# Moving later loads to the GpSimd queue, and the transposes of q and k behind those of u, in an attention and MLP-mixer kernel

## The chip, the cores and the metric

The kernel runs on one core of one Trainium2 chip. The metric is the device time of one execution in microseconds (us). A single core has no second die to compare with, so a run counts as slow here when it is over 1.5% above the fastest of the same kernel; only fast runs are compared. The kernels were run in rounds that alternate with the kernel before on the same chip. Runs of different experiments can come from different chips; a ratio always compares with the kernel before in the same rounds. TensorE, VectorE, ScalarE, GpSimd and SyncE appear in the profile as PE, DVE, ACT, POOL and SP; PEld is TensorE's weight load, and a q behind a name (SPq, ACTq) means work of that engine's sequencer, such as issuing a DMA.

## The reference, cut to what matters

Windowed attention with 4 sink keys, then an MLP mixer, on 4 batches. Everything is float32 outside and bf16 inside.

```python
# q, k, v: (4 batches, 8 heads, 768, 64); n_sink = 4, window = 128
scores = q @ k.T / 8, kept where key < 4 or 0 <= query - key < 128
x = softmax(scores) @ v                      # heads side by side: (4, 768, 512)
u = x + (relu(x.T @ w_tok1) @ w_tok2).T      # tokens:   768 -> 256 -> 768
out = u + relu(u @ w_ch1) @ w_ch2            # channels: 512 -> 1536 -> 512
```

## The kernel before

The batches are pipelined. While TensorE does the channel products of batch b (`ch1`, `ch2`: the "main" stream), the attention and the token products of batch b + 1 are put in between (the "fill"), each at a fraction of the main stream's length. A batch has two groups of four heads, so groups 0 to 7; batch 1 is groups 2 and 3, batch 2 groups 4 and 5, batch 3 groups 6 and 7. From batch 1 on, u is transposed by six DMA transposes (128 x 512 bf16, 128 KB each), and from batch 2 on q and k of each group by one DMA transpose each (128 x 1536 bf16, 384 KB). In this text a "stage" is the stretch of one batch's main stream. All of the following go through the sync queue, where the traces show them issued in program order (in the kernel before the transposes of u, whose input was written by 92.9 us, were issued from 112.6 us on, behind the six loads issued from 91.1 to 109.0): loads of groups 4 to 7, all DMA transposes, and all stores but one.

```python
def load_qk(eng, src, dst, G, lo, hi): ...
    # groups 4 to 7: one DMA of 768 KB, rows of 64 floats (256 bytes), 3072 rows
    eng.dma_start(out=dst.rearrange("p h t d -> p (h t) d"),
                  in_=src[G.b, G.h0:G.h0 + GH].rearrange("h (t p) d -> p (h t) d", p=P))

def cast_and_turn(G, which, copy):           # groups 4 to 7
    ...                                      # GpSimd casts q or k to bf16
    T = att.tile([P, 2 * NT, P], BF16, name="qT" if which == 0 else "kT")
    nc.sync.dma_start_transpose(out=T, in_=flat)

def utr(st):                                 # u of batch 1, 2, 3
    nc.sync.dma_start_transpose(out=uT[:, :, ts(st, P)], in_=u_sb[:, st])

def ch1(half, ft):                           # first product of a stage: needs uT of st 0, 1, 2
    ps = ps_mx.tile([P, HS], FP32, name="ps_v", tag="mx")   # two PSUM buffers
    for c in range(NC):
        nc.tensor.matmul(ps, w_ch1[:, c, ts(ft, P)], uT[:, c, ds(half * HS, HS)], ...)
    # even ft: ScalarE empties PSUM, odd ft: VectorE

# ---- cut ----
def fetch(g):                                # on the sync queue
    G = held[g] = tiles(g)
    load_q(G, 0, GH); load_k(G, 0, GH); load_v(G)

def prep_v(g):
    cast_v(held[g])                          # GpSimd; frees the buffer that v of g + 2 needs
    if g + 2 < NG and g >= 2:
        fetch(g + 2)

# ---- cut: the fill of stage b, for batch b + 1 (groups g, h) ----
    lo, mid = (0.36, 0.80) if b == 0 else (0.02, 0.68)      # attention of batch b + 1
    ...
    if b + 2 < B:
        fill += [(mid + 0.01, lambda n=n: prep_qk(n)) for n in (h + 1, h + 2)]   # cast and turn
        fill += [(mid + 0.01, lambda n=n: prep_v(n)) for n in (h + 1, h + 2)]    # cast, then fetch
    hi = mid + 0.03                                         # u of batch b + 1 and its transposes
    fill += [(hi + (0.97 - hi) * n / (len(nhead) - 1), f) for n, (f, _) in enumerate(nhead)]
```

The attention of batches 2 and 3 begins with four small copies on ScalarE (`sink_keys`, L225 before, L229 after), which read kT of both groups before the first exponential.

The softmax here doesn't subtract the row's maximum and nothing guards it: scores larger than these inputs give would overflow.

Of the kernel before, what the change touches and what calls it, by code (L numbers as in the profile page):

```python
# [16 lines left out]
def kernel(  # L17
# [13 lines left out]
    nc = tc.nc  # L31
# [75 lines left out]
    def load_q(G, lo, hi, eng=nc.sync):  # L107
        return load_qk(eng, q, G.q32, G, lo, hi)
# [5 lines left out]
        src, dst = ((G.q32, G.qb), (G.k32, G.kb))[which]  # L114
        copy(dst[:, j].rearrange("p t i d -> p i t d"), src[:, 2 * j:2 * j + 2])

    def cast_and_turn(G, which, copy):
        src, dst = ((G.q32, G.qb), (G.k32, G.kb))[which]
        flat = dst.rearrange("p j t i d -> p (j t i d)")
        copy(flat.rearrange("p (t h d) -> p t h d", t=NT, h=GH), src.rearrange("p h t d -> p t h d"))  # L120
        T = att.tile([P, 2 * NT, P], BF16, name="qT" if which == 0 else "kT")
        nc.sync.dma_start_transpose(out=T, in_=flat)  # L122
        G.T[which] = [T.rearrange("d (t j) p -> d t j p", j=2)[:, :, j] for j in range(2)]

    def by_dve(o, i):
# [5 lines left out]
    def by_act(o, i):  # L131
        nc.scalar.activation(o, i, AF.Copy)

    def load_v(G):
        return nc.sync.dma_start(out=G.v32.rearrange("p h t d -> p (h t) d"),  # L135
                                 in_=v[G.b, G.h0:G.h0 + GH].rearrange("h (t p) d -> p (h t) d", p=P))

    def load_sinks():
# [179 lines left out]
    def mixer(b, x_b):  # L318
        h1 = mix.tile([P, NTOK, DM], BF16, name="h1")
        u_sb = mix.tile([P, NT, DM], BF16, name="u_sb")  # L320
        uT = mix.tile([P, NC, S], BF16, name="uT")
        v1 = mix.tile([P, NF, S], BF16, name="v1", bufs=1)
        st_ps = {}

        def tok1(a, tt):
            ps = ps_mx.tile([P, GH * D], FP32, name="ps_h", tag="mx")
            for t in range(NT):
                nc.tensor.matmul(ps, w_tok1[:, t, ts(tt, P)], x_b[:, t, ds(a * GH * D, GH * D)],  # L328
                                 start=(t == 0), stop=(t == NT - 1))
            nc.scalar.activation(h1[:, tt, ds(a * GH * D, GH * D)], ps, AF.Relu)  # L330

        def tok2(st):
            ps = ps_ms.tile([P, DM], FP32, name="ps_u", tag="ms")
            for tt in range(NTOK):
                nc.tensor.matmul(ps, w_tok2[:, tt, ts(st, P)], h1[:, tt], start=(tt == 0), stop=(tt == NTOK - 1))  # L335
            nc.vector.tensor_tensor(out=u_sb[:, st], in0=ps, in1=x_b[:, st], op=ALU.add)  # L336

        def utr(st):
            if b > 0:
                nc.sync.dma_start_transpose(out=uT[:, :, ts(st, P)], in_=u_sb[:, st])  # L340
                return
            ps = ps_ms.tile([P, NC, P], BF16, name="ps_ut", tag="ms")
            for c in range(NC):
                nc.tensor.transpose(ps[:, c], u_sb[:, st, ts(c, P)], ident)
            nc.scalar.activation(uT[:, :, ts(st, P)], ps, AF.Copy)

        def ch1(half, ft):
            ps = ps_mx.tile([P, HS], FP32, name="ps_v", tag="mx")
            for c in range(NC):
                nc.tensor.matmul(ps, w_ch1[:, c, ts(ft, P)], uT[:, c, ds(half * HS, HS)],  # L350
                                 start=(c == 0), stop=(c == NC - 1))
            if ft % 2 == 0:
                nc.scalar.activation(v1[:, ft, ds(half * HS, HS)], ps, AF.Relu)  # L353
            else:
                nc.vector.tensor_scalar(out=v1[:, ft, ds(half * HS, HS)], in0=ps, scalar1=0.0, scalar2=None, op0=ALU.max)  # L355

        def ch2(st, part):
            if part == 0:
                st_ps[st] = ps_mx.tile([P, DM], FP32, name="ps_w", tag="mx")
            ps = st_ps[st]  # L360
            for ft in range(4 * part, 4 * part + 4):
                nc.tensor.matmul(ps, v1[:, ft, ts(st, P)], w_ch2[:, ft], start=(ft == 0), stop=(ft == NF - 1))  # L362
            if part == NF // 4 - 1:
                o = osb.tile([P, DM], FP32, name="o")
                nc.vector.tensor_tensor(out=o, in0=ps, in1=u_sb[:, st], op=ALU.add)  # L365
                if b == B - 1 and st == NT - 1:
                    hw = DM // 2
                    nc.sync.dma_start(out=out[b, ds(st * P, P), 0:hw], in_=o[:, 0:hw])
                    nc.scalar.dma_start(out=out[b, ds(st * P, P), hw:DM], in_=o[:, hw:DM])
                else:  # L370
                    nc.sync.dma_start(out=out[b, ds(st * P, P)], in_=o)  # L371

        t1 = [[(lambda a=a, tt=tt: tok1(a, tt), 660) for tt in range(NTOK)] for a in range(GB)]
        T2 = lambda st: (lambda: tok2(st), 432)
        X = lambda st: (lambda: utr(st), 222)
        C1 = lambda h, f: (lambda: ch1(h, f), 650)
        C2 = lambda s, p: (lambda: ch2(s, p), 864)
        head = [T2(0), T2(1), X(0), T2(2), X(1), T2(3), X(2), T2(4), X(3), T2(5), X(4), X(5)]
        if b == 0:
            hf = NF // 2  # L380
            m = [T2(0), T2(1), X(0), T2(2), X(1), X(2), C1(0, 0), T2(3), C1(0, 1), X(3), T2(4), C1(0, 2), X(4), T2(5),
                 C1(0, 3), X(5)]
            m += [C1(0, f) for f in range(4, hf)] + [C1(1, f) for f in range(hf)]
            m += [C1(0, f) for f in range(hf, NF)] + [C1(1, f) for f in range(hf, NF)]
            m += [C2(s, p) for s in range(NT) for p in range(NF // 4)]
        else:
            m = [C1(0, f) for f in range(NF)]
            for n in range(3):
                m += [C1(1, f) for f in range(4 * n, 4 * n + 4)] + [C2(n, p) for p in range(NF // 4)]
            m += [C2(s, p) for s in range(3, NT) for p in range(NF // 4)]  # L390
        return t1, head, m
# [17 lines left out]
    with tc.manual_schedule():  # L409
# [4 lines left out]
            mixers[b] = mixer(b, xs[b])  # L414

        def fetch(g):
            G = held[g] = tiles(g)
            load_q(G, 0, GH)
            load_k(G, 0, GH)
            load_v(G)  # L420

        def prep_qk(g, by=(by_pool, by_pool)):
            if held[g].dma:
                for which in range(2):
                    cast_and_turn(held[g], which, by_pool)
                return
            for j in range(2):
                for which in range(2):
                    cast(held[g], j, which, by[which])

        def prep_v(g):
            cast_v(held[g])
            if g + 2 < NG and g >= 2:
                fetch(g + 2)

        def begin(g):
            parts[g] = attention(g, held[g], xs[g // GB], False)
# [40 lines left out]
        def more_loads():  # L478
            load_ch1(0)
            load_ch1(1)  # L480
            G = held[2] = tiles(2)
            load_q(G, 0, GH, nc.gpsimd)
            load_k(G, 0, GH, nc.gpsimd)
            load_ch2(0)
            load_ch2(1)
            G = held[3] = tiles(3)
            load_q(G, 0, GH, nc.gpsimd)
            last = load_k(G, 0, GH, nc.gpsimd)
            after(load_v(held[2]), last)
            load_v(G)  # L490

        idle(11)
        seq = [C(G0, 0, 0, by_dve), C(G0, 0, 1, by_act), zeros, step(0, 0, 0), step(0, 0, 1), I(1), step(0, 1, 0)]
        seq += [C(G0, 1, 0, by_pool), C(G0, 1, 1, by_pool), step(0, 0, 2), step(0, 1, 1), step(0, 0, 3), step(0, 1, 2)]
        seq += [C(G1, 0, 0, by_pool), C(G1, 0, 1, by_pool), I(1), step(0, 1, 3), step(1, 0, 0), step(0, 1, 4)]
        seq += [step(1, 0, 1), step(0, 1, 5), step(1, 1, 0)]
        seq += [C(G1, 1, 0, by_pool), C(G1, 1, 1, by_pool), step(0, 2, 0), step(1, 0, 2), step(1, 1, 1), step(1, 0, 3)]
        seq += [lambda: cast_v(G0), lambda: cast_sinks(0, GB), step(1, 1, 2), load_tok, step(1, 1, 3)]
        seq += [step(0, 3, 0), step(1, 1, 4), step(0, 3, 1), lambda: cast_v(G1), step(0, 3, 2), step(1, 2, 0)]
        seq += [step(1, 1, 5), step(0, 3, 3), step(0, 3, 4), step(0, 3, 5), more_loads, step(1, 4, 0)]  # L500
        seq += [f for f, _ in mixers[0][0][0]]
        seq += [step(1, 4, 1), step(1, 4, 2)]
        seq += [f for f, _ in mixers[0][0][1]]
        seq += [build_mask0, lambda: cast_sinks(GB, NG)]
        run(seq)

        for b in range(B):
            main, fill = mixers.pop(b)[2], []
            if b + 1 < B:
# [2 lines left out]
                nt1, nhead, _ = mixers[b + 1]  # L512
                order = []
                if b == 0:
                    order += [(lambda: prep_qk(2), 0)]
                order += [(lambda g=g: begin(g), 0)] + ([(lambda h=h: begin(h), 0)] if b > 0 else [])
                if held[g].dma:
# [15 lines left out]
                    order += [(step(g, 3, 2 * n), 6), (step(g, 3, 2 * n + 1), 6)]  # L533
                order += [(step(h, 2, 0), 8)] + [(f, 7) for f, _ in nt1[0]]
                order += [(step(h, 3, i), 6) for i in range(NT)] + [(f, 7) for f, _ in nt1[1]]
                lo, mid = (0.36, 0.80) if b == 0 else (0.02, 0.68)
                total, t = sum(w for _, w in order), 0
                for f, w in order:
                    fill.append((lo + (mid - lo) * t / total, f))
                    t += w  # L540
                if b + 2 < B:
                    fill += [(mid + 0.01, lambda n=n: prep_qk(n)) for n in (h + 1, h + 2)]
                    fill += [(mid + 0.01, lambda n=n: prep_v(n)) for n in (h + 1, h + 2)]
                hi = mid + 0.03
                fill += [(hi + (0.97 - hi) * n / (len(nhead) - 1), f) for n, (f, _) in enumerate(nhead)]
            run(spread(main, fill))
# [1 line left out]
_INS = ['q', 'k', 'v', 'n_sink', 'window', 'moe_w_tok1', 'moe_w_tok2', 'moe_w_ch1', 'moe_w_ch2']  # L548
# [31 lines left out]
```

## Time and profile before

| | before |
|---|---|
| median of the runs | 257.0 us (255.64 to 260.06, one of four slow) |
| span of the profiled run | 256.6 us |
| TensorE busy | 210.2 us, 82% |
| one TensorE wait for uT in stage 1 | 24.6 us |
| mean granted TensorE clock | 0.93 |

The first fence is from the page of the kernel before: the span, TensorE's busy time, then rows of 40 slices of 6.4 us each (the digit is the busy share in tenths; PEclk is the granted clock, DMA the mean busy share of the 16 DMA engines), then the DMA queues with packets, MB and the share of the engines' time. q1 is the queue of SyncE (hardware, as the page calls it), q0 that of GpSimd (software).

```profile
span 256.6 us, 3888 instructions
...
PE   8996859997998960005888999979799999999993
...
PEclk9999968999999997555999999997999999999999
DMA  6999999599499999997100149550001115401122
...
q1 hardware_dynamic: 76560, 26.22, 49.1%
q0 software_dynamic: 4576, 7.11, 12.6%
```

There is one large hole in TensorE's row, almost four slices wide (24.6 us), and the DMA row is nearly full in it. The list of waits of the kernel before (who waited for whom: us in total, times, longest) names it:

```profile
PE ps_v L350 <- DMA uT<-u_sb: 24.6, 1, 24.6
```

The timeline of the sync queue in the kernel before (start us, us, what) shows why uT is late. L122 are transposes of q and k, L103 and L135 loads, L371 a store, L340 the transposes of u:

```profile
83.30 1.78 SPq L122 DMA_TRANSPOSE qT<-qb  x1
...
89.36 1.64 SPq L122 DMA_TRANSPOSE kT<-kb  x1
91.06 0.98 SPq L103 DMA_DIRECT2D q_1248<-in_q_dram  x1
92.09 2.54 SPq L103 DMA_DIRECT2D k_1249<-in_k_dram  x1
94.73 3.47 SPq L135 DMA_DIRECT2D v_1252<-in_v_dram  x1
...
105.50 3.50 SPq L135 DMA_DIRECT2D v_1263<-in_v_dram  x1
109.09 3.46 SPq L371 DMA_DIRECT2D out_dram<-o  x1
112.64 2.52 SPq L340 DMA_TRANSPOSE uT<-u_sb  x2
...
115.84 5.15 SPq L340 DMA_TRANSPOSE uT<-u_sb  x4
```

VectorE wrote the last u of batch 1 by 92.9 us, but six loads of groups 6 and 7 stand in the queue ahead of its transposes. The view of the tile uT in the kernel before (from 85 to 130 us; first the issue times in ns, minimum, median and maximum) shows that the transposes themselves are quick:

```profile
L340 SPq DMA_TRANSPOSE uT<-u_sb x6: 1211/1216/1264, 112.6 to 119.8; - x6
...
DMA to landing us min/median/max: 2.4/2.5/3.8
```

The timeline of GpSimd in the kernel before, around the cast of v of group 3 (L200) and the masks of group 3 (L252 to L262):

```profile
67.48 1.46 POOL L200 CAST va<-v_470 128x1536 bf16<-128x1536 f32 x1
68.91 1.15 POOL L252 TENSOR_TENSOR pT<-pT,mask_92 128x512 bf16<-128x512 bf16 x1
...
76.49 0.64 POOL L262 TENSOR_SCALAR_AFFINE_SELECT pT<-pT 128x512 bf16<-128x512 bf16 x1
```

TensorE's attention output of group 3 (L280) starts at 77.25 us, 0.1 us behind the last mask: GpSimd has hardly any slack there.

### The profile page before, as it was taken

What the parts mean: (1) busy time and instruction counts of PE and PEld (TensorE: products, weight loads), DVE (VectorE), ACT (ScalarE), POOL (GpSimd) and SP (SyncE); (2) the same over time, 40 slices, a digit from 0 to 9 for tenths busy, and PEclk for the clock granted to TensorE, in tenths of its full rate; (3) what the DMA queues carried; (4) which work ended last, traced back from release to release, by engine and by line L of the source; (5) the groups of instructions that cost most, each with busy time, mean ns of one, the idle gap of its engine ahead of it and who ended that gap; (6) DMA issues with size and microseconds to landing.
All of it is one profiled execution on the core that took longest, in us unless ns stands there. A gap on an engine that the chain in (4) does not pass through costs nothing.

```text
span 256.6 us, 3888 instructions
## 1 busy us (share of the span) xinstructions
PE 210.2 (82%) x1547; PEld 112.7 (44%) x1565; DVE 107.0 (42%) x241; ACT 91.1 (36%) x152; POOL 91.1 (36%) x121
## 2 busy tenths in 40 slices
PE   8996859997998960005888999979799999999993
PEld 3444624554565520002445665434456644554441
DVE  5657644364746450000225473531344636333221
ACT  3794224469751000002775421065754200231100
POOL 8759322018999300000485980015654000000000
PEclk9999968999999997555999999997999999999999
DMA  6999999599499999997100149550001115401122
GB/s 231 320 195 178 233 293 260 183 210 228 94 216 229 241 212 218 218 231 160 43 0 3 41 96 191 147 143 0 3 0 43 41 43 135 111 0 43 41 82 82
DMA packets 82113, 34.88 MB, mean 136 GB/s; under 512 B 72544, under 2 KB 78432, under 8 KB 82096
## 3 DMA queue, kind: packets, MB, share of 16 engines
q1 hardware_dynamic: 76560, 26.22, 49.1%
q0 software_dynamic: 4576, 7.11, 12.6%
q10 hardware_dynamic: 960, 1.31, 1.5%
q8 instruction: 12, 0.20, 0.3%
q14 instruction: 5, 0.04, 0.1%
HBM read 26.77 MB, written 6.29 MB: 129 GB/s over the span
## 4 chain that ended last, share of the span: by engine, by line
PE 57%; SPq 12%; ACT 10%; DVE 8%; DMA 6%; POOL 3%; issue 2%; DVEq 0%; ACTq 0%; POOLq 0%
PE ps_v L350 20%; PE ps_w L362 18%; ACT pT L248 7%; SPq L103 4%; DMA v_948<-in_v_dram 4%; PE ps_s L242 3%; PE ps_u L335 3%; SPq L135 3%; PE ps_h L328 3%; DMA uT<-u_sb 2%; PE ps_warm L468 2%; SPq L122 2%; SPq L371 2%; PE ps_tr L211 2%; SPq L340 2%
## 5 line engine op out<-in xcount | busy, mean ns | idle before, releaser
L350 PE MATMUL ps_v<-uT,w_ch_104 128*128 128x384 bf16 x384 | 77.6, 338 | 31.1 <-DMA uT<-u_sb 24.6
L350 PEld LDWEIGHTS <-w_ch_104 128*128 128x128 bf16 x384 | 36.6, 100 | 62.8 <-issue 42.9
L248 ACT ACTIVATE pT<-ps_s 128x1024 bf16<-128x1024 f32 (+1 forms) x48 | 43.6, 957 | 8.5 <-PE ps_s L242 7.8
L252 POOL TENSOR_TENSOR pT<-pT,mask_92 128x512 bf16<-128x512 bf16 x12 | 13.8, 1153 | 74.8 <-ACT pT L248 74.8
L365 DVE TENSOR_TENSOR o<-ps_w,u_sb 128x512 f32<-128x512 f32 x24 | 16.6, 692 | 22.0 <-PE ps_w L362 22.0
L336 DVE TENSOR_TENSOR u_sb<-ps_u,x_b 128x512 bf16<-128x512 f32 x24 | 16.3, 687 | 18.3 <-PE ps_u L335 17.0
L259 POOL TENSOR_SCALAR_AFFINE_SELECT pT<-pT 128x640 bf16<-128x640 bf16 x24 | 18.3, 764 | 13.8 <-ACT pT L248 13.8
L355 DVE TENSOR_SCALAR v_584<-ps_v 128x384 bf16<-128x384 f32 x12 | 6.7, 557 | 38.9 <-PE ps_v L350 38.9
L353 ACT ACTIVATE v_584<-ps_v 128x384 bf16<-128x384 f32 x12 | 5.9, 494 | 42.7 <-PE ps_v L350 42.6
L293 DVE TENSOR_TENSOR x_b<-ps_o,rc 128x256 bf16<-128x256 f32 x42 | 17.8, 425 | 1.5
L362 PE MATMUL ps_w<-w_ch_105,v_584 128*128 128x512 bf16 x69 | 17.5, 379 | 0.2
L362 PE MATMUL ps_w<-w_ch_105,v_1341 128*128 128x512 bf16 x69 | 17.5, 379 | 0.2
L362 PE MATMUL ps_w<-w_ch_105,v_112 128*128 128x512 bf16 x68 | 17.3, 379 | 0.2
L242 PE MATMUL ps_s<-qT,kT 64*128 64x256 bf16 x192 | 16.0, 275 | 1.3 <-ACT pT L248 0.8
L353 ACT ACTIVATE v_1922<-ps_v 128x384 bf16<-128x384 f32 x12 | 5.9, 491 | 29.7 <-PE ps_v L350 16.2
L362 PE MATMUL ps_w<-w_ch_105,v_1922 128*128 128x512 bf16 x70 | 15.9, 379 | 0.1
L262 POOL TENSOR_SCALAR_AFFINE_SELECT pT<-pT 128x512 bf16<-128x512 bf16 x24 | 15.6, 650 | 0.0
L280 PEld LDWEIGHTS <-pT 128*128 128x128 bf16 x192 | 14.3, 98 | 2.8 <-issue 0.4
L280 PE MATMUL ps_o<-va,pT 128*128 128x65 bf16 x168 | 14.9, 194 | 0.0
L292 DVE RECIPROCAL rc<-ps_o 128x4 f32<-128x4 f32 x42 | 7.5, 179 | 17.1 <-PE ps_o L284 10.5
L328 PE MATMUL ps_h<-x_b,w_tok_102 128*128 128x256 bf16 x96 | 13.4, 272 | 1.0 <-DVE x_b L293 0.5
L353 ACT ACTIVATE v_1341<-ps_v 128x384 bf16<-128x384 f32 x12 | 5.9, 493 | 22.3 <-DVE o L365 13.4
(130 smaller groups left out, 271.6 us busy)
## 6 DMA issues: line engine op xcount, KB each, us to landing
out_dram<-o SPq DMA_DIRECT2D x23, 256.0 KB, 2.2
w_ch_104<-in_moe_w_ch_dram POOLq DMA_DIRECT2D x2, 768.0 KB, 9.3
w_ch_105<-in_moe_w_ch_dram POOLq DMA_DIRECT2D x2, 768.0 KB, 18.8
k_114<-in_k_dram ACTq DMA_DIRECT2D x2, 384.0 KB, 5.6
q_113<-in_q_dram SPq DMA_DIRECT2D x2, 384.0 KB, 4.9
q_119<-in_q_dram SPq DMA_DIRECT2D x2, 384.0 KB, 8.3
v_117<-in_v_dram SPq DMA_DIRECT2D x1, 768.0 KB, 10.6
v_123<-in_v_dram SPq DMA_DIRECT2D x1, 768.0 KB, 13.7
```

Of the source, the lines that this page charges most:

```text
L242: nc.tensor.matmul(ps[:, i, at:at + w].rearrange("p (c q) -> p c q", q=P), G.T[1][j][ds(64 * i, 64), kt], G.T[0][j][ds(64 * i, 64), kt:kt ...
L248: nc.scalar.activation(pT[:, :, 512 * u:512 * u + n], ps[:, :, 0:n], AF.Exp, scale=scale)
L259: nc.gpsimd.affine_select(out=cur, in_=cur, compare_op=ALU.is_ge, fill=0.0, base=0, pattern=[[0, NT - 1], [1, P]], channel_multiplier=-1)
L262: nc.gpsimd.affine_select(out=prv, in_=prv, compare_op=ALU.is_ge, fill=0.0, base=-1, pattern=[[0, NT - 2], [-1, P]], channel_multiplier=1)
L280: nc.tensor.matmul(o, pT[:, i, ds(256 * qt, P)], G.va[:, h, qt], start=(qt < 2 and h == 0), stop=(h == GH - 1 and qt == 0), skip_group_che ...
L293: nc.vector.tensor_tensor(out=x_b[:, qt, c0:c0 + GH * D].rearrange("p (h d) -> p h d", h=GH), in0=o[:, :, 0:D], in1=rc.to_broadcast([P, GH ...
L328: nc.tensor.matmul(ps, w_tok1[:, t, ts(tt, P)], x_b[:, t, ds(a * GH * D, GH * D)], start=(t == 0), stop=(t == NT - 1))
L336: nc.vector.tensor_tensor(out=u_sb[:, st], in0=ps, in1=x_b[:, st], op=ALU.add)
L350: nc.tensor.matmul(ps, w_ch1[:, c, ts(ft, P)], uT[:, c, ds(half * HS, HS)], start=(c == 0), stop=(c == NC - 1))
L353: nc.scalar.activation(v1[:, ft, ds(half * HS, HS)], ps, AF.Relu)
L362: nc.tensor.matmul(ps, v1[:, ft, ts(st, P)], w_ch2[:, ft], start=(ft == 0), stop=(ft == NF - 1))
L365: nc.vector.tensor_tensor(out=o, in0=ps, in1=u_sb[:, st], op=ALU.add)
```

## The change

The intent is to take the loads out of the way of the transposes of u. Loads of groups 4 to 7 (and v of groups 2 and 3) go to GpSimd's queue; the transposes of q and k for the next batch but one are put behind those of u, at 0.98 of the stage, and the attention starts at 0.12 instead of 0.02 to give them time. Besides, the start of the kernel is rearranged: casts of sink values earlier or later, the token products of batch 0 in the other PSUM pool.

```diff
-    def cast_and_turn(G, which, copy):
+    def cast_all(G, which, copy):            # the cast alone
+    def turn(G, which):                      # the transpose alone, on the sync queue
 ...
-    def load_v(G):
-        return nc.sync.dma_start(...)
+    def load_v(G, eng=nc.sync):
+        return eng.dma_start(...)
 ...                                          # token products of batch 0
-            ps = ps_ms.tile([P, DM], FP32, name="ps_u", tag="ms")
+            ps = (ps_mx if b == 0 else ps_ms).tile([P, DM], FP32, name="ps_u", tag="mx" if b == 0 else "ms")
 ...
         def fetch(g):
-            G = held[g] = tiles(g)
-            load_q(G, 0, GH)
-            load_k(G, 0, GH)
-            load_v(G)
+            if g < NG:
+                G = held[g] = tiles(g)
+                load_q(G, 0, GH, nc.gpsimd)
+                load_k(G, 0, GH, nc.gpsimd)
+                load_v(G, nc.gpsimd)
 ...                                          # start: mask and sink casts
-        seq += [build_mask0, lambda: cast_sinks(GB, NG)]
+                    fill += [(0.15, build_mask0), (0.2, lambda: cast_sinks(GB, NG))]
 ...
-                lo, mid = (0.36, 0.80) if b == 0 else (0.02, 0.68)
+                lo, mid = (0.36, 0.80) if b == 0 else (0.12, 0.70)
 ...
-                hi = mid + 0.03
-                fill += [(hi + (0.97 - hi) * n / (len(nhead) - 1), f) for n, (f, _) in enumerate(nhead)]
+                hi = mid + 0.02
+                fill += [(hi + (0.93 - hi) * n / (len(nhead) - 1), f) for n, (f, _) in enumerate(nhead)]
+                fill += [(0.98, lambda n=n: turn_qk(n)) for n in nxt]
```

(Cut: the order of the first operations of batch 0, and v of groups 2 and 3 on GpSimd's queue. Every later line number is 4 higher, or 9 higher from the middle of the kernel on.)

More of the change, by code (lines that the diff above doesn't have):

```diff
@@ L115, in cast, with flat @@
         copy(dst[:, j].rearrange("p t i d -> p i t d"), src[:, 2 * j:2 * j + 2])
-    def cast_and_turn(G, which, copy):
-        src, dst = ((G.q32, G.qb), (G.k32, G.kb))[which]
-        flat = dst.rearrange("p j t i d -> p (j t i d)")
-        copy(flat.rearrange("p (t h d) -> p t h d", t=NT, h=GH), src.rearrange("p h t d -> p t h d"))
+    def flat(G, which):
+        return (G.qb, G.kb)[which].rearrange("p j t i d -> p (j t i d)")
+    def cast_all(G, which, copy):
+        copy(flat(G, which).rearrange("p (t h d) -> p t h d", t=NT, h=GH),
+             (G.q32, G.k32)[which].rearrange("p h t d -> p t h d"))
+    def turn(G, which):
         T = att.tile([P, 2 * NT, P], BF16, name="qT" if which == 0 else "kT")
-        nc.sync.dma_start_transpose(out=T, in_=flat)
+        nc.sync.dma_start_transpose(out=T, in_=flat(G, which))
         G.T[which] = [T.rearrange("d (t j) p -> d t j p", j=2)[:, :, j] for j in range(2)]
@@ L132, in by_act @@
         nc.scalar.activation(o, i, AF.Copy)
-    def load_v(G):
-        return nc.sync.dma_start(out=G.v32.rearrange("p h t d -> p (h t) d"),
+    def load_v(G, eng=nc.sync):
+        return eng.dma_start(out=G.v32.rearrange("p h t d -> p (h t) d"),
                                  in_=v[G.b, G.h0:G.h0 + GH].rearrange("h (t p) d -> p (h t) d", p=P))
@@ L380, in mixer @@
             hf = NF // 2
-            m = [T2(0), T2(1), X(0), T2(2), X(1), X(2), C1(0, 0), T2(3), C1(0, 1), X(3), T2(4), C1(0, 2), X(4), T2(5),
+            m = [T2(0), T2(1), T2(2), X(0), X(1), X(2), C1(0, 0), T2(3), C1(0, 1), X(3), T2(4), C1(0, 2), X(4), T2(5),
                  C1(0, 3), X(5)]
@@ L416, in fetch @@
         def fetch(g):
-            G = held[g] = tiles(g)
-            load_q(G, 0, GH)
-            load_k(G, 0, GH)
-            load_v(G)
+            if g < NG:
[3 more added lines that the diff above has]
+                load_v(G, nc.gpsimd)
         def prep_qk(g, by=(by_pool, by_pool)):
-            if held[g].dma:
-                for which in range(2):
-                    cast_and_turn(held[g], which, by_pool)
+            G = held[g]
+            if G.dma:
+                cast_all(G, 0, by_pool)
+                cast_all(G, 1, by_pool)
                 return
@@ L428, in prep_qk, with turn_qk @@
                 for which in range(2):
-                    cast(held[g], j, which, by[which])
+                    cast(G, j, which, by[which])
         def prep_v(g):
             cast_v(held[g])
-            if g + 2 < NG and g >= 2:
-                fetch(g + 2)
+            fetch(g + 2)
+        def turn_qk(g):
+            turn(held[g], 0)
+            turn(held[g], 1)
         def begin(g):
@@ L487, in more_loads @@
             load_q(G, 0, GH, nc.gpsimd)
-            last = load_k(G, 0, GH, nc.gpsimd)
-            after(load_v(held[2]), last)
-            load_v(G)
+            load_k(G, 0, GH, nc.gpsimd)
+            load_v(held[2], nc.gpsimd)
+            load_v(G, nc.gpsimd)
         idle(11)
@@ L496 @@
         seq += [step(1, 0, 1), step(0, 1, 5), step(1, 1, 0)]
-        seq += [C(G1, 1, 0, by_pool), C(G1, 1, 1, by_pool), step(0, 2, 0), step(1, 0, 2), step(1, 1, 1), step(1, 0, 3)]
-        seq += [lambda: cast_v(G0), lambda: cast_sinks(0, GB), step(1, 1, 2), load_tok, step(1, 1, 3)]
+        seq += [lambda: cast_sinks(0, GB), C(G1, 1, 0, by_pool), C(G1, 1, 1, by_pool), step(0, 2, 0), step(1, 0, 2), step(1, 1, 1), step(1, 0, 3)]
+        seq += [lambda: cast_v(G0), step(1, 1, 2), load_tok, step(1, 1, 3)]
         seq += [step(0, 3, 0), step(1, 1, 4), step(0, 3, 1), lambda: cast_v(G1), step(0, 3, 2), step(1, 2, 0)]
@@ L540 @@
                     t += w
-                if b + 2 < B:
-                    fill += [(mid + 0.01, lambda n=n: prep_qk(n)) for n in (h + 1, h + 2)]
-                    fill += [(mid + 0.01, lambda n=n: prep_v(n)) for n in (h + 1, h + 2)]
-                hi = mid + 0.03
-                fill += [(hi + (0.97 - hi) * n / (len(nhead) - 1), f) for n, (f, _) in enumerate(nhead)]
+                nxt = (h + 1, h + 2) if b + 2 < B else ()
+                fill += [(mid + 0.01, lambda n=n: prep_qk(n)) for n in nxt]
+                fill += [(mid + 0.01, lambda n=n: prep_v(n)) for n in nxt]
+                hi = mid + 0.02
+                fill += [(hi + (0.93 - hi) * n / (len(nhead) - 1), f) for n, (f, _) in enumerate(nhead)]
+                fill += [(0.98, lambda n=n: turn_qk(n)) for n in nxt]
             run(spread(main, fill))
```

## The prediction

> **What bounds the kernel now.** TensorE carries the time: busy 210.2 of 256.6 us (engine table). Its one large hole is in the waits by pair: 24.6 us, once, of the first up-projection of batch 1 (L350) for the DMA that transposes u. The table of stretches gives 92 to 118 us: TensorE 1.9 us busy of 26, DMA share over 1. The sync queue's own timeline says why: between 91.1 and 109.0 us it issues six 768 KB loads of groups 6 and 7 at 3.5 us each, and only from 112.6 us the transposes of u, although the last u_sb of batch 1 was written at 92.9 us. The loads pace at the DMA rate (768 KB in 3.5 us, about 220 GB/s, 256-byte rows).
>
> **Removed, moved, added.**
> 1. Start: sink casts earlier, mask and later sink casts out of the stretch 29.7 to 33.1 us (VectorE timeline), tok2 in the other PSUM pool. First up-projection at about 34.8 instead of 37.5 us, with the sink casts: -3 us.
> 2. The sync queue no longer holds loads. The wait for uT falls from 24.6 to about 2 us: -22.
> 3. The loads go to GpSimd. Its issues of 256, 512 and 768 rows took 0.73, 0.78 and 0.86 us; extrapolated to 3072 rows about 1.5 us (estimate). Six such issues, about 9 us, now stand between the two casts of v (66.0 and 67.5 us) and the masks of group 3 (68.9 to 77.1 us), and the attention output of group 3 starts at 77.25 us, right behind those masks. So about 9 us of GpSimd time lands on the chain: +8. The loads of groups 4 and 5, which began at 52 us, begin at about 64.
> 4. The transposes of q and k (four per batch, 8.0 us of issue from 150.9 us, last landing about 11 us after the first issue) come after the last store of the batch. All four are needed: ScalarE copies the sink keys of both groups before the first exponential. Moving attention from 2% to 12% hides only about 3.7 us. In batch 2 I expect TensorE to wait about 8 us more than now (first for kT, then for ScalarE to free PSUM): +7. In batch 1 the loads of groups 6 and 7 still run [...] The exponentials of batch 1 may start at 108 to 122 us, against 122.2: +7 to +15.
>
> Sum: -3 -22 +8 +7 +7 to +15, so -3 to +5, before the doubt. Items 3 and 4 are estimates that may be too dark (sharing mild, fewer waits coinciding), so I set the middle lower: 253 us, eighty per cent from 240 to 265. Faster by over 2%: 0.42; within 2%: 0.37; slower: 0.21.
>
> **What would show it.** 2: the 24.6 us wait gone; sync queue without loads, transposes of u right behind u_sb. 3: six GpSimd issues of about 1.5 us before the masks of group 3; a TensorE wait of 6 to 9 us at the attention output (L280) of group 3. 4: in the waits, ScalarE's sink-key copies (L225) waiting for DMA kT in batches 1 and 2, several us each, and TensorE scores waiting for kT or qT. 1: first up-projection at about 35 us.
>
> **What would make it wrong.** GpSimd issues far shorter or longer than 1.5 us (12 of them, half on the chain); transposes that keep their 1.2 to 2.8 us pace beside loads (then 240 to 245) or are starved by them (then over 262); a PE clock that stays low after new waits.

The trace showed a DMA share of 1.28 from 92 to 118 us, where the loads run. The clock in the last line is a risk read from the trace: in the kernel before, behind the wait of 24.6 us, the granted clock was 0.54 from 120 to 123 us and 1.00 from 123 to 126 us.

## The result, and the profile after

| | before | after |
|---|---|---|
| median of the runs | 257.0 us | 274.94 us (272.76 to 278.19, one of four slow) |
| ratio of the fast runs | 1 | 1.069 (95% interval 1.059 to 1.078) |
| span of the profiled run | 256.6 us | 273.3 us |
| TensorE busy, for the same 1547 instructions | 210.2 us | 215.6 us |
| mean granted TensorE clock | 0.93 | 0.91 |
| TensorE wait for uT in stage 1 | 24.6 us | 25.5 us |

A ratio here is the mean time of one kernel's fast runs over that of the other's of the same rounds, so it is not quite the ratio of the medians.

The change made the kernel 7% slower. The same views of the kernel after follow. First its page:

```profile
span 273.3 us, 3883 instructions
...
PE   8998685988938960006778999995799999999994
...
PEclk9999997999997995555959999997799999999999
DMA  6999999900799699999900110569001103601122
...
q0 software_dynamic: 7488, 18.12, 30.0%
q1 hardware_dynamic: 33328, 15.21, 25.7%
```

The hole in TensorE's row is still there. The software queue moved 18.12 MB in 7488 packets, so its packets are large (2420 bytes on average), while those of the hardware queue are small (456 bytes).

The list of waits of the kernel after, its lines for uT, kT and the masks:

```profile
PE ps_v L354 <- DMA uT<-u_sb: 25.5, 1, 25.5
...
ACT ks_97 L229 <- DMA kT<-kb: 6.6, 2, 3.7
...
PE ps_o L284 <- POOL pT L256: 4.7, 2, 3.4
```

The timeline of the sync queue in the kernel after. No load stands in front of the transposes of u (L344), and they are issued from 93.84 us on, 19 us earlier than before. But they crawl:

```profile
93.84 13.56 SPq L344 DMA_TRANSPOSE uT<-u_sb  x4
107.49 0.53 SPq L375 DMA_DIRECT2D out_dram<-o  x1
108.07 13.26 SPq L344 DMA_TRANSPOSE uT<-u_sb  x2
121.43 0.53 SPq L375 DMA_DIRECT2D out_dram<-o  x1
122.06 4.73 SPq L126 DMA_TRANSPOSE qT<-qb  x1
...
130.89 1.79 SPq L126 DMA_TRANSPOSE kT<-kb  x1
```

The view of the tile uT in the kernel after, from 85 to 130 us: up to 10.6 us to issue one, and 8.6 to 28.0 us to land, against 2.4 to 3.8 before.

```profile
L344 SPq DMA_TRANSPOSE uT<-u_sb x6: 1286/2338/10625, 93.8 to 118.8; - x6
...
DMA to landing us min/median/max: 8.6/18.0/28.0
```

The timeline of GpSimd in the kernel after: six issues of 1.42 to 1.46 us (two are shown) stand around the cast of v of group 3 and ahead of its masks, which start at 77.36 instead of 68.91 us.

```profile
67.38 1.46 POOL L103 DMA_DIRECT2D q_933<-in_q_dram  x1
...
75.92 1.42 POOL L139 DMA_DIRECT2D v_948<-in_v_dram  x1
77.36 1.16 POOL L256 TENSOR_TENSOR pT<-pT,mask_92 128x512 bf16<-128x512 bf16 x1
```

Milestones of TensorE's timeline, in us from the start of the span, show where the 16.7 us came from:

| | before | after | later by | added in this step |
|---|---|---|---|---|
| first PE transpose of group 2 (stage 0, middle) | 51.44 | 51.40 | 0.0 | 0.0 |
| end of the last product of stage 0 | 93.9 | 100.0 | 6.1 | +6.1 |
| first product of stage 1 (has uT) | 118.53 | 125.52 | 7.0 | +0.9 |
| first product of stage 2 | 168.21 | 180.45 | 12.2 | +5.2 |
| first product of stage 3 | 218.77 | 235.56 | 16.8 | +4.6 |
| end | 256.6 | 273.3 | 16.7 | -0.1 |

So the change added costs in three places (up to the end of stage 0, in stage 1 and in stage 2; the experiments put them down to GpSimd's issues and to the order of q and k, for stage 1 by analogy only) and gained nothing at the wait for uT, where it was to gain 22 us. Not all of the last two steps is waiting. For nearly the same matmuls (348 and 350 records in both kernels) TensorE was busy 49.9 instead of 47.4 us in stage 1, at a granted clock of 0.90 instead of 0.96, and 49.1 instead of 47.1 us in stage 2, at 0.94 instead of 0.97.

### The profile page after: what moved, and what is told of

Its sections match the earlier page's. It is cut to its first block, busy times and chain, and to the rows that moved or that the text cites. A ratio compares the mean times of both kernels' runs of the same rounds, so it can differ in the third digit from the quotient of the medians.

```text
span 273.3 us, 3883 instructions
## 1 busy us (share of the span) xinstructions
PE 215.6 (79%) x1547; PEld 114.9 (42%) x1565; DVE 107.0 (39%) x241; ACT 90.7 (33%) x152; POOL 110.5 (40%) x135
## 3 DMA queue, kind: packets, MB, share of 16 engines
q0 software_dynamic: 7488, 18.12, 30.0%
## 4 chain that ended last, share of the span: by engine, by line
PE 51%; SPq 13%; POOL 9%; DMA 8%; DVE 7%; ACT 7%; issue 4%; POOLq 0%; DVEq 0%; ACTq 0%
PE ps_w L366 21%; PE ps_v L354 15%; SPq L344 7%; SPq L126 5%; ACT pT L252 5%; DMA w_ch_104<-in_moe_w_ch_dram 4%; DMA kT<-kb 3%; PE ps_u L339 3%; PE ps_s L246 3%; DVE o L369 2%; PE ps_warm L477 2%; PE ps_h L332 2%; POOL pT L263 2%; POOL pT L266 1%; DVE x_b L297 1%
## 5 line engine op out<-in xcount | busy, mean ns | idle before, releaser
L354 PE MATMUL ps_v<-uT,w_ch_104 128*128 128x384 bf16 x384 | 81.6, 352 | 33.0 <-DMA uT<-u_sb 25.5
L354 PEld LDWEIGHTS <-w_ch_104 128*128 128x128 bf16 x384 | 37.8, 104 | 67.7 <-DMA uT<-u_sb 26.0
L340 DVE TENSOR_TENSOR u_sb<-ps_u,x_b 128x512 bf16<-128x512 f32 x24 | 16.3, 687 | 17.5 <-PE ps_u L339 17.4
L357 ACT ACTIVATE v_572<-ps_v 128x384 bf16<-128x384 f32 x12 | 5.8, 494 | 45.1 <-PE ps_v L354 45.1
L366 PE MATMUL ps_w<-w_ch_105,v_112 128*128 128x512 bf16 x69 | 18.4, 394 | 0.2
L366 PE MATMUL ps_w<-w_ch_105,v_1341 128*128 128x512 bf16 x68 | 17.4, 379 | 0.2
L366 PE MATMUL ps_w<-w_ch_105,v_572 128*128 128x512 bf16 x68 | 17.4, 379 | 0.2
L366 PE MATMUL ps_w<-w_ch_105,v_1922 128*128 128x512 bf16 x70 | 15.9, 379 | 0.1
L357 ACT ACTIVATE v_1922<-ps_v 128x384 bf16<-128x384 f32 x12 | 5.9, 490 | 28.7 <-PE ps_v L354 16.3
L246 PEld LDWEIGHTS <-kT 64*128 64x128 bf16 x192 | 7.2, 96 | 19.4 <-issue 13.2
L296 DVE RECIPROCAL rc<-ps_o 128x4 f32<-128x4 f32 x42 | 7.5, 178 | 19.6 <-PE ps_o L284 10.0
## 6 DMA issues: line engine op xcount, KB each, us to landing
v_123<-in_v_dram SPq DMA_DIRECT2D x1, 768.0 KB, 13.5
```

The lines of the kernel that those rows point to most:

```text
L246: nc.tensor.matmul(ps[:, i, at:at + w].rearrange("p (c q) -> p c q", q=P), G.T[1][j][ds(64 * i, 64), kt], G.T[0][j][ds(64 * i, 64), kt:kt ...
L340: nc.vector.tensor_tensor(out=u_sb[:, st], in0=ps, in1=x_b[:, st], op=ALU.add)
L366: nc.tensor.matmul(ps, v1[:, ft, ts(st, P)], w_ch2[:, ft], start=(ft == 0), stop=(ft == NF - 1))
```

## The experiments

My theory after reading the result, theory A: the loads of groups 6 and 7 on the software queue starve the transposes (these get so small a share of the DMA engines that they crawl), because of the size of their packets. A packet is one record of a DMA engine's work in the profile; in the kernel after a load packet has 4096 bytes, a transpose packet 256, and from 100 to 118 us 870 of the former took 315 ns each, 997 of the latter 34 ns. Rivals: B, the wait comes from the order on the sync queue; C, any loads of these bytes slow the transposes as much; D, the software queue as such is the cause and not the size of its packets.

### 1. No load beside the transposes

The kernel after, with the loads of groups 6 and 7 on the sync queue behind all transposes of batch 1 (so that none is in flight beside those of u):

```diff
-            fetch(g + 2)
+            if g + 2 not in (6, 7):
+                fetch(g + 2)
 ...
                 fill += [(0.98, lambda n=n: turn_qk(n)) for n in nxt]
+                if b == 0:
+                    fill += [(0.99, lambda n=n: late_fetch(n)) for n in (6, 7)]   # on nc.sync
```

> The kernel after, with one thing changed: the six loads of groups 6 and 7 go to the sync queue behind all transposes of batch 1, so that no load is in flight while u, q and k of batch 1 are transposed. Theory A (loads on the software queue starve the transposes, [...] a load packet has 4096 bytes, a transpose packet 256): the transposes of u are issued in about 1.2 us each and land in 2.4 to 4 us, the TensorE wait for uT falls from 25.5 to under 4 us, and the time from 275 to 246 to 254 us. Rival B (the wait comes from the order on the sync queue, stores and transposes in front of one another): wait and time stay within 3 us of the kernel after.

Measured: 250.2 us (249.16 to 251.6), ratio to before 0.968. Tile uT of this run, from 85 to 130 us; the view lists no wait for uT at all:

```profile
L344 SPq DMA_TRANSPOSE uT<-u_sb x6: 1206/1219/1309, 94.0 to 101.2; - x6
DMA to landing us min/median/max: 2.4/2.4/2.5
```

Theory A's numbers came true and B's did not: with the order of the transposes unchanged and only the loads gone from beside them, the wait of 25.5 us is gone and so are 24.7 us of time (274.94 to 250.2). That the loads beside the transposes cause the wait is shown by this; by what mechanism, the other experiments ask.

### 2. The same loads, from a hardware queue in small packets

```diff
-                load_q(G, 0, GH, nc.gpsimd)      # and k, v
+                eng = nc.gpsimd if g < 6 else nc.scalar
+                load_q(G, 0, GH, eng)            # and k, v
```

> The kernel after, with the six loads of groups 6 and 7 issued from ScalarE's hardware queue instead of GpSimd, at the same place, so that as many bytes run beside the transposes but in 256-byte packets. Theory A (size of the packets): the transposes of u land in 3 to 7 us instead of 8.6 to 28, the wait for uT is under 12 us. Rival C (any six loads of 4.7 MB beside the transposes slow them so): they land in 15 us or more, wait for uT 20 us or more. The whole time decides nothing, since ScalarE is held up by its own issues (about 3.5 us each), expected 255 to 270.

Measured: 264.4 us (263.3 and 265.51). Tile uT of this run:

```profile
  DMA uT<-u_sb: 5.6, 1
DMA to landing us min/median/max: 5.2/9.0/10.0
```

The wait is 5.6 us against 25.5, where C expected 20 or more. This does not settle C, though: ScalarE issued so slowly (its third load from 99.15 us, its fourth from 106.97) that the packets of only two of its six loads (1.6 of 4.7 MB, counted in the trace) had run when the wait ended at 105.6 us, so fewer bytes ran beside the transposes than intended. Experiments 13 and 14 settle it below. The landing times are longer than I expected (5.2 to 10.0, not 3 to 7). The total says nothing, as expected: ScalarE then held TensorE up for 12.5 us because it was itself busy issuing.

### 3. One part of the change alone: only the loads

The kernel before, with `fetch` on GpSimd's queue and nothing else:

```diff
-            load_q(G, 0, GH)
-            load_k(G, 0, GH)
-            load_v(G)
+            load_q(G, 0, GH, nc.gpsimd)
+            load_k(G, 0, GH, nc.gpsimd)
+            load_v(G, nc.gpsimd)
```

> The kernel before with only the loads of groups 4 to 7 moved to the GpSimd queue; order of transposes, positions and start as before. Theory A: the transposes of q, k and then u all run beside the loads, so the wait for uT stays over 20 us, and the masks of group 3 are late by about 8.5 us as in the kernel after: 265 to 280 us. Rival B: with q and k not behind u, 245 to 258 us.

Measured: 265.08 us (one of four slow), ratio 1.024, at the lower edge of what A expected. The wait for uT is 27.6 us. The sync queue of this run shows who is starved here: the transposes of q and k, which come first, and u waits behind them.

```profile
95.55 24.34 SPq L122 DMA_TRANSPOSE kT<-kb  x1
```

### 4. The rest of the change: everything but the loads

The kernel after with all those loads back on the sync queue:

```diff
-                load_q(G, 0, GH, nc.gpsimd)      # and k, v; also v of groups 2 and 3
+                load_q(G, 0, GH)
```

> The kernel after with all loads of groups 4 to 7 (and v of groups 2 and 3) back on the sync queue; transposes of q and k behind u, positions and start as in the kernel after. Both theories: wait for uT about 24 us again as in before; masks of group 3 not late; the q and k transposes behind u cost about 5 us in batch 1 and 5 us in batch 2: 263 to 272 us. If it is below 259, the reorder of the transposes costs nothing.

Measured: 260.85 us, ratio 1.010, below what I expected. The wait for uT is 16.9 us, not 24: the four transposes of q and k, which took the queue from 83.3 to 91.0 us in the kernel before, no longer stand in front. ScalarE's waits for kT (13.5 us in all, none before) give that back and more. So the rest of the change, the reorder and the new start together, costs about 1% (95% interval 0.4 to 1.5%), the loads alone 2.4% (1.6 to 3.2%), and both together 6.9%. The parts are not additive: my reading is that with the loads alone, q and k pay for the starving and are there when u is, while with both, u is starved first, and q and k still have to be transposed after it.

### 5. The kernel before, with the loads put behind the transposes

If the loads need only be out of the way, no other queue is needed. The kernel before with two edits:

```diff
-            if g + 2 < NG and g >= 2:
+            if g + 2 < 6:
                 fetch(g + 2)
 ...
+                if b == 0:
+                    fill += [(0.98, lambda n=n: fetch(n)) for n in (6, 7)]
```

> The kernel before with one thing changed: the six loads of groups 6 and 7 stay on the sync queue but stand behind the transposes of u and the last store of batch 0. Theory A and its corollary (what held up batch 1 in the kernel before was only that these loads were issued, and run, ahead of the transposes of u): wait for uT from 24.6 to under 3 us, transposes of u landing in 2.4 to 4 us, 229 to 236 us, and no new wait of the casts of groups 6 and 7 over 2 us. If another wait takes its place: over 240 us.

Measured: 237.14 us (236.77 to 239.39), ratio 0.922, one us above the band. The wait for uT is 4.0 us and not under 3, because the transposes of q and k still hold the queue until 91.1 us. The transposes of u land in 2.4 to 3.1 us. From its list of waits:

```profile
PE ps_v L350 <- DMA uT<-u_sb: 4.0, 1, 4.0
```

### 6. Half of the loads beside the transposes

As experiment 1, but only group 7 is moved; the three loads of group 6 stay on GpSimd's queue (`for n in (7,)`).

> The kernel after with only the loads of group 7 moved behind the transposes; those of group 6 (half of the 4.7 MB) stay on the GpSimd queue beside them. Theory A: the transposes of u run freely once the three loads are through, so the wait for uT is between those of the kernel after (25.5) and of the run with all six moved (none over 1 us): 7 to 14 us; time 255 to 264 us.

Measured: 264.33 us (263.38 and 265.29); wait for uT 15.4 us, just over the band of 7 to 14 but between none (no load) and 25.5 us (six loads). Transposes landed in 4.6 to 19.6 us. The time is 0.3 us over its band (255 to 264).

### 7. What GpSimd's issues cost

Experiment 1, with the loads of groups 4 and 5 on the sync queue as well:

```diff
-                load_q(G, 0, GH, nc.gpsimd)      # and k, v; also v of groups 2 and 3
+                load_q(G, 0, GH)
```

> The run with loads of groups 6 and 7 behind the transposes (250.2 us), with the remaining loads too (groups 4 and 5, v of 2 and 3) back on the sync queue, so that GpSimd issues no 3072-row load. If the six issues of 1.42 us ahead of the masks of group 3 cost what I read (waits of 4.7 us for these masks and about 1 us of slow clock): wait of the attention output on GpSimd gone, 243 to 247 us. If GpSimd's issues cost nothing: 249 to 251.

Measured: 243.27 us (243.1 to 243.79), ratio 0.944. The wait of the attention output on GpSimd (4.7 us) is gone from the list, and 6.9 us of time with it (250.2 to 243.27). That is about what the milestone "end of stage 0" lost (6.1 us). A part may be the clock: in the profiled runs 2.1 us of the lead were there before the six issues ahead of the masks (first PE transpose of group 2 at 48.88 against 50.95 us, at a granted clock of 1.00 against 0.86 from 40 to 52 us).

### 8. What the order of q and k costs in batch 2

Experiment 1, with the transposes of q and k for batch 2 back at their old place, ahead of those of u; no load runs in that stage:

```diff
+                if b == 1:
+                    fill += [(mid + 0.01, lambda n=n: turn_qk(n)) for n in nxt]
 ...
-                fill += [(0.98, lambda n=n: turn_qk(n)) for n in nxt]
                 if b == 0:
+                    fill += [(0.98, lambda n=n: turn_qk(n)) for n in nxt]
```

> The run with loads of groups 6 and 7 behind the transposes (250.2 us), with the transposes of q and k for batch 2 back where the kernel before had them, just behind their casts and ahead of those of u; those for batch 1 stay behind. The order costs about 5 us in batch 2 (ScalarE waits for kT about 7 us there): 243 to 247 us, and ScalarE's waits for kT fall from 14.6 to about 8 us. If the order is free: 249 to 251.

Measured: 245.86 us (245.58 to 246.56), ratio 0.954, 4.3 us less than experiment 1 (3.6 by the ratios). In the profiles stage 2 took 49.0 instead of 53.9 us, and its granted clock was 1.00 instead of 0.94, with TensorE busy 45.8 instead of 48.2 us: the slower matmuls went away with the waits. The list of waits of experiment 1 has

```profile
ACT ks L229 <- DMA kT<-kb: 14.6, 4, 4.5
```

and that of this run

```profile
ACT ks L229 <- DMA kT<-kb: 8.5, 2, 4.5
```

One batch's two waits of ScalarE for kT are gone. The reason is in the program order: at 0.98 no product of the stage is left, so the transposes of q and k are queued behind the last store, which waits for the last product of the stage (stage 1 of the kernel after: last product to 180.6 us, store issued at 181.66, the four transposes from 182.29 to 189.4); 0.10 of a stage more before the attention, about 5.5 us of its 55, does not cover the 7.1 us of four transposes.

### 9 to 11. Putting the pieces together

All three start from experiment 5. The first adds the start of the kernel after, the second makes its mask and later sink casts on GpSimd, which is idle then (from 39.8 to 57.1 us in the kernel before), and the third also puts the two transposes of group 5 behind the first three of u:

```diff
# 9: the start of the kernel after (PSUM pool and order of the token products, sink casts, mask)
# 10
-        nc.vector.memset(mask0, 1.0)
+        nc.gpsimd.memset(mask0, 1.0)             # and its second memset
-        fill += [(0.15, build_mask0), (0.2, lambda: cast_sinks(GB, NG))]
+        fill += [(0.15, build_mask0), (0.2, lambda: cast_sinks(GB, NG, nc.gpsimd))]
# 11
                 for n, (f, _) in enumerate(nhead):
                     fill.append((hi + (0.97 - hi) * n / (len(nhead) - 1), f))
+                    if b == 0 and n == 6:        # behind the third transpose of u
+                        fill += [(fill[-1][0], lambda w=w: turn_one(held[5], w)) for w in range(2)]
```

> The kernel before with loads of groups 6 and 7 behind the transposes of u (237.1 us), plus the start of the kernel after alone (sink casts earlier, mask and later sink casts put off into the up-projections, token products of batch 0 in the other PSUM pool). My reading of the kernel after: the first up-projection comes 3.7 us earlier (33.7 instead of 37.5), but the mask and sink casts then hold VectorE from about 39 to 44.5 us and TensorE waits for it, so that at 51.5 us nothing is left: 236 to 238 us. If the start's gain lasts, as I predicted: 233 to 235.

> The same, with the mask and the later sink casts made on GpSimd, which is idle from about 40 to 57 us, instead of VectorE. If VectorE's block is what ate the gain: TensorE does not wait for VectorE there, 233 to 236 us. If the up-projections up to 51 us are held by something else (casts of q and k, the loads): 236 to 238.

> The run before this one, with the two transposes of group 5 moved behind the first three transposes of u (those of group 4 stay ahead). The remaining wait of 4.0 us for uT in batch 1 comes from the transposes of q and k ahead of u on the sync queue: wait for uT under 1.5 us, no wait for kT over 1 us, 2 to 4 us less than the run before this one. If kT of group 5 is then late: ScalarE waits for it and nothing is gained.

| run | median (six runs, all fast) | ratio to before | wait for uT |
|---|---|---|---|
| 9 | 235.44 us (234.05 to 235.7) | 0.912 | 4.1 us |
| 10 | 232.72 us (231.91 to 234.33) | 0.905 | 5.5 us |
| 11 | 231.21 us (230.69 to 232.13) | 0.898 | 1.4 us |

In run 9 my expectation was too dark: some of the start's gain lasts. Its first up-projection comes at 33.6 instead of 37.5 us, VectorE is held by mask and sink casts until 44.4 us and TensorE waits 1.5 us for it, and by 51 us a lead of about 2.2 us is left (an up-projection that began at 53.50 us in experiment 5 begins at 51.21). In run 10 that wait is gone, and the lead is larger. Run 11 took 1.5 us instead of the 2 to 4 expected: the wait for uT fell to 1.4 us, but ScalarE now waits 2.3 us for kT. Run 11 is the fastest version found; it beats the kernel before by 10%.

### 12 to 14. Packet size or queue?

Three runs of the kernel after that load groups 6 and 7 in other row lengths. Their outputs are wrong, which doesn't matter for the times. The values of batch 3 are scrambled; bytes, shapes and the rest of the program are the same. The first uses ScalarE's hardware queue and 6144-byte rows, the others GpSimd's queue and rows of 512 and 1536 bytes:

```diff
# 12
+    nc.scalar.dma_start(out=t.rearrange("p h t d -> p (h t d)"),
+                        in_=s[...].rearrange("h (a t) d -> (h a) (t d)", a=P // GH))
# 13 (n = 2), 14 (n = 6)
+    nc.gpsimd.dma_start(out=t.rearrange("p h (t n) d -> p h t (n d)", n=n),
+                        in_=s[...].rearrange("h (t p n) d -> p h t (n d)", p=P, n=n))
```

> The run with the loads of groups 6 and 7 on ScalarE's hardware queue, with the same bytes loaded in 128 rows of 6144 bytes instead of 3072 of 256 (wrong result on purpose: the batches 3's q, k and v are scrambled; times and shapes are the same). Theory A (size of the load packets, whatever queue they come from): [...]the first transposes of u land in 10 us or more, wait for uT 9 to 18 us. Rival D (it is the software queue that starves the hardware queue, not the size): transposes of u land as with the 256-byte rows on ScalarE's queue (5 to 10 us) or sooner, wait for uT under 6 us.

> The kernel after with the loads of groups 6 and 7 still on the GpSimd queue at the same place and of the same bytes, but in rows of 512 bytes (wrong result on purpose: batch 3 is scrambled), which that queue should move in packets of 512 instead of 4096 bytes. Theory A (packet size): [...]wait for uT 2 to 8 us instead of 25.5. Rival D (the software queue as such starves the hardware queue): 15 us or more.

> The same with rows of 1536 bytes. Theory A: between the two: [...]wait for uT 6 to 15 us. Rival D: 15 us or more, no different from rows of 512 bytes.

Medians (two runs each): 263.0, 262.67 and 259.04 us. Tile uT of the three runs, first the wait, then the landing times. Run 12:

```profile
  DMA uT<-u_sb: 12.2, 1
DMA to landing us min/median/max: 6.5/12.3/16.3
```

Run 13:

```profile
  DMA uT<-u_sb: 14.2, 1
DMA to landing us min/median/max: 3.5/13.1/18.5
```

Run 14:

```profile
  DMA uT<-u_sb: 9.8, 1
DMA to landing us min/median/max: 2.9/10.5/13.6
```

To read these, I counted DMA packets in the traces while loads and transposes of batch 1 ran side by side:

```
run                          stretch, us   load packets (bytes, mean ns)   transpose packets of 256 bytes
1  no load beside            96 to 103     none                            2502
after                        100 to 118    870 (4096, 315)                  997
3  loads alone on GpSimd     95 to 115     945 (4096, 328)                 1307
6  half of the loads         94 to 106     457 (4096, 339)                  489
13 rows of 512 bytes         100 to 110    654 (4096, 229)                  684
14 rows of 1536 bytes        100 to 104    317 (4608 or 3072, 188)          348
2  ScalarE queue, 256 bytes  100 to 118   7037 (256, 25)                   5469
12 ScalarE queue, 6144 bytes  98 to 110    162 (6144, 616)                 1368
```

In experiments 13 and 14 the edit failed at its purpose: the software queue's packets had about 4 KB again (4096 bytes with rows of 512, 4608 or 3072 with rows of 1536), so the size could not be varied there, and the wait under 8 us that A expected of run 13 did not come; nor did the 15 us or more that D expected of both. They still tell something. Nearly all of the 4.7 MB ran beside the transposes in them as in the kernel after, and the wait was 14.2 and 9.8 us instead of 25.5: so bytes alone do not set the wait, and rival C is out. The wait (25.5, 14.2 and 9.8 us) falls with the time of one load packet (315, 229 and 188 ns).

In the stretches counted, where the loads of the software queue run steadily, close to one transpose packet passed per load packet in every run (1.0 to 1.4). Why is not shown: the counts are over all engines, and the packed traces name no DMA engine, so the order of single packets on one engine could not be looked at. The loads are about 1060 to 1150 packets and the transposes of u 3072, so the loads run out first, and the first product followed their end: the last load packet began at 124.6, 112.5 and 108.2 us, the product at 125.5, 114.1 and 109.8 us (kernel after, runs 13 and 14).

Outside these stretches the counts are different. In the kernel after, from 118 to 124 us, 518 transpose packets passed beside 53 load packets, but all queues together moved only 69 GB/s (212 from 100 to 118 us); what held them for these 6 us of the wait is not known. In run 2 the ratio of 0.8 is a mean over a stretch longer than the wait: while the product waited, from 98 to 104 us, it was 0.3 (987 transpose packets, 3031 load packets).

Run 12 does not fit that count. Beside the 6144-byte packets of ScalarE's hardware queue the transposes were late too (6.5 to 16.3 us to land, against 2.4 to 2.5 in run 1): the wait of 12.2 us is in A's band and above D's 6 us. But the first transpose landed in 6.5 us and not in the 10 or more that A expected, and eight transpose packets passed per load packet (1368 and 162) and not about one. Both kinds of packet were slow there: a load packet took 616 ns (about 240 to 280 from 94 to 98 us, without transposes), a transpose packet 88 ns (20 in run 1). Nor is it a clean comparison with run 2: four of its six loads (3.1 MB) had run when the wait ended, the other two were issued only at 111.6 us. So it stays open how much of the 25.5 us is the size of the packets and how much the software queue as such. What is shown is that the loads beside the transposes delay them (experiments 1 and 6: a wait of 25.5 us with six loads, 15.4 with three, none without), that it is not by their bytes alone (13 and 14: 14.2 and 9.8 us with the same bytes), and that 1.0 to 1.4 transpose packets passed per load packet while the software queue's loads ran steadily.

## Why the prediction was right or wrong

The result, 274.94 us, is above the range of 240 to 265 us, and the direction that I held most likely (faster) was wrong.

- **Step 2 failed: "The wait for uT falls from 24.6 to about 2 us: -22."** It stayed: 25.5 us. The issue order did change as I said, the sync queue held no loads and the transposes of u were issued from 93.84 us. I took their 1.2 us each from a stretch without loads beside them. Beside the loads on GpSimd's queue they took up to 10.6 us to issue and up to 28.0 us to land. Experiment 1 shows the step's size: with no load beside, the wait is gone and the kernel is 24.7 us faster. I had named the risk ("or are starved by them (then over 262)") but gave it little room. That the loads beside them did it is shown; by what mechanism is open (experiments 12 to 14).
- **Step 3 was right.** The issues took 1.42 to 1.47 us (I had extrapolated 1.5), the masks of group 3 came 8.45 us later, and the end of stage 0 lost 6.1 us (I had +8); TensorE's own wait for the masks was 4.7 us (I had 6 to 9). Experiment 7 gives 6.9 us back when they are taken away, a part of which may be the clock.
- **Step 4 was right in mechanism.** ScalarE's sink-key copies wait for kT (9.7 us in three waits, 3.7 the longest). Batch 2 lost 4.6 us by the milestones and 4.3 by experiment 8 (I had +7). Batch 1 lost 5.2 us (I had +7 to +15); what I thought would make it dearer, loads beside q and k, had mostly passed by the time q and k were transposed (the last load packet began at 124.6 us, the four transposes were issued from 122.06 to 132.7), because the loads had starved u first. In both batches about 2 to 2.5 us of the loss are longer matmuls at a lower granted clock (0.90 and 0.94 instead of 0.96 and 0.97), which I had named only as a risk.
- **Step 1 was half right.** The first up-projection came at 33.7 us (I had 34.8), but by 51.4 us the kernel after had no lead left (I had -3). Experiments 9 and 10 show the start's gain when VectorE is not held up by the deferred casts. In experiment 9 a lead of 2.2 us survives with the same casts on VectorE; the kernel after lost even that. Its granted clock was lower there (0.86 between 40 and 52 us, against 1.00 in experiment 9 from 30 to 52 us), and experiments 4 and 7, which up to there issue the same (they ran on two chips), show what that is worth: the 24 up-projections before the first PE transpose of group 2 took 5.9 us in the one, at a clock of 0.67 (46 to 50 us), and 4.4 us in the other, at 1.00. In the kernel after TensorE also waited 2.9 us for VectorE, against 1.5 in experiment 9. What lowered the clock is not known.
- **The sum.** With the measured terms, 0 at the start, +6.1 for GpSimd, +0.9 for uT, +5.2 and +4.6 for q and k, it is +16.8 us, which is the profiled difference of 16.7. Mine was -3 to +5, and I then shifted the middle to 253 us on the hope that steps 3 and 4 were too dark. They were, by some us; step 2 was wrong by 23.

## What to carry to other kernels

Loads sent through another queue can still run beside what was behind them in the old one. Here they did: u's transposes took 8.6 to 28.0 us to land beside the loads of GpSimd's queue, 2.4 to 2.5 without loads beside them (experiment 1). So ask what will run beside what, and count packets as well as bytes (870 load packets of 4096 bytes, 997 transpose packets of 256, from 100 to 118 us). Here the short urgent transposes were better protected by issuing the bulk loads after them in the same queue (experiment 5: two edits, 8% faster) than by moving the loads to another queue (experiment 3: 2.4% slower; with the rest of the change 7%). And the transposes of q and k behind the last store of a stage were issued only when the stage's last product was done (to 180.6 us; they from 182.29), so what the next stage needs first does not belong there.

Times measured here, for the next estimate: a DMA transpose of 128 x 512 bf16 without loads beside it took 1.2 to 1.3 us to issue (experiment 1); one of 128 x 1536 took 1.5 to 2.8 us in the kernel before. A load on GpSimd took 0.73 us to issue for 256 rows, 0.75 to 0.83 for 512, 0.87 to 0.88 for 768 and 1.42 to 1.47 for 3072, and in the kernel after its mask work began only behind the six issues (77.36 instead of 68.91 us).
